# Eight attention heads and a squared-ReLU layer on one core: block products for one chunk more, scales for two passes at a time, and a planner with new numbers

## The chip, the core and the metric

The kernel runs on one core of one Trainium2 chip. The metric is the device time of one execution in microseconds. The core has a tensor engine (PE, whose weight loads, PEld, overlap its matmuls), a vector engine (DVE), a scalar engine (ACT), GpSimd (POOL) and a sync engine (SP), which here does nothing but issue DMAs. Each engine takes its instructions in the order in which the program lists them.

## The reference

Eight batches of eight heads of 576 tokens with 64 numbers each go through block-causal attention. What comes out, 4608 tokens of 512 numbers, goes through a two-layer network with a squared ReLU.

```python
scores = scale * np.matmul(q, k.transpose(0, 1, 3, 2))
mask = (pos[:, None] // 64) >= (pos[None, :] // 64)
scores = np.where(mask, scores, -1000000000.0)
scores = scores - np.max(scores, axis=-1, keepdims=True)
attn = np.exp(scores)
attn = attn / (np.sum(attn, axis=-1, keepdims=True) + 1e-09)
x = np.matmul(attn, v)            # then (8 * 576, 512)
h = x @ w_in                      # 512 -> 2048
r = np.maximum(h, 0.0)
out = (r * r) @ w_out             # 2048 -> 512
```

Everything is float32. The kernel gets near that from float16 matmuls: a number is split into a high and a low float16 part, and a product takes three matmuls (high with high, high with low, low with high).

## The kernel before, in words

**Attention.** The work is cut into 40 passes of one batch and two heads: 8 short ones (batches 0 and 1, the first three blocks of 64 queries), 8 for the other six blocks of those batches, and 24 whole ones (batches 2 to 7). For each group of query blocks a pass does scores on PE (A, tile `side`), the negated row maximum on DVE (B, `nmx`), the exponential on ACT (C, `p`, with its row sum `sm`), the sum's scaling on POOL (S), the reciprocal on DVE (R, `rs`), and the scaled rows with their split (H and L, `p_rows`), which DMAs (T) turn into `p_turned`. The product with v (G, PE, `px`) and a copy out on ACT (X, `x32`) end it. The first 12 passes (`WHOLE`) take v in float32. From the thirteenth pass on v is split too, and for that each pass finds a power of two: `front` (line 522) sums |v| along each row on ACT (fv, tile `st`), transposes the sums on PE (fa, `pm`), takes the maximum on DVE (fb, `top`), spreads it over the partitions with a matmul (fc), masks it on DVE (fd, `m`), makes the scales on POOL (fe, three instructions), and ACT and DVE write the high and low halves (vh, vl, `v16`). These tasks are put into the plan from line 1661 on; one task `load` issues the DMAs for a pass's queries, keys and values.

**The network.** The 4608 tokens are 12 chunks of 384, in the order 0, 1, 2, 4, 3, 5, 7, 6, 8, 10, 9, 11 (`turn_of`, line 781). A chunk's x is normalised (hb, xm: squares, a sum by matmul `nq`, a power of two) and split into `xt_all`. Then the first layer comes in one of two forms, which `plain(ck)` and `PLAIN` (lines 32 and 783) choose:

- The first four chunks of the order are plain (`unit`, line 932): 16 units, each of 12 matmuls with 384 columns into a PSUM tile `pair`; then a relu (pos), a square (sqr), the cast to the high half of `hidden` (top) and the remainder, its low half (rem).
- The other eight are made by block products (`group_steps`, line 1028): weights and x are cut in 2 x 2 blocks and combined as in Strassen's and Winograd's scheme, so that seven products stand for eight. There are 4 groups of 7 products, each of 12 matmuls with 192 columns into tiles `group`. Copies (c, ACT or DVE) and adds (a, DVE) put the products together in tiles `r`; then square, cast and remainder as above. A square on DVE is one instruction, on ACT two (relu, then square; for `r21`, which comes from a relu, one). The weights' combinations are made once, by `turn_steps` (line 979): for each quarter 18 steps, 10 adds and 4 remainders on POOL or DVE, 4 casts on ACT. They stand in `turned_w` and, some, in place of blocks of `w1`, so the last five steps of a quarter wait for the last plain chunk's first layer (line 1601).

The second layer (`out_steps`, line 1144) is 144 matmuls with 512 columns for each chunk, 48 for 128 tokens, in tiles `pair` or `po`; the output is scaled (ob, one instruction on DVE or two on ACT) and stored.

**Weights.** Both matrices arrive as float32 words and pass through a chain for each of 16 slices: bits (POOL), prelu (ACT, tile `wt`), join (DVE), a maximum (DVE for the first, ACT for the second), then the cast (ACT, DVE or POOL) and the low half (DVE). All of that runs beside the first passes and chunk 0.

**The order of the work.** `Plan` (line 152) decides it before anything runs. Every task has one or more engines with a cost in ns for each, the tasks it waits for, rings of buffers that it takes and frees, and a rank. `run` steps through a model of time: of the tasks that could start first on the engine that comes free first it takes the one with the lowest rank. Where a task may go to several engines, it takes the one with the lowest sum of start and cost:

```python
cost = at + queues[q] + (EASE + (SPARE if name[0] in "Dc" and "POOL" in queues else 0) if q == "DVE" else 0)
```

`DRAGS` (line 155) is by how much a task on POOL holds up DVE in that model. The constants of lines 34 to 74 and the table `SHIFTS` (line 100) move ranks. The order that comes out is written down through the helper `Queue`, whose line 124 therefore stands in every row of the profile (125 after the change): rows are told apart by tiles.

Of the kernel before, what the change touches and what calls it, by code (L numbers as in the profile page):

```python
# [19 lines left out]
P = 128  # L20
D = 64
# [10 lines left out]
PLAIN = 4  # L32
ALONE = 14
CALM = 1195.46
# [19 lines left out]
W0 = (-248.45, 10.9, 139.39, 8.21, 175.27, 11.63, 23.26)  # L54
W1 = (-30.45, -241.86, -561.58, -723.11, -96.62)
NORMS = (-3.68, -3.62)
YR = (90.87, 1.94, 1.28, -9.6)
UR = (225.07, 13.43, 15.26)
LATER = 16
EASE = 61.67  # L60
SPARE = 157.67
SLACK = 0
EARLY = 542.67
BEGIN = 281.87
FILLER = 10000
CHAIN = 488.46
FRONT = 95.73
# [4 lines left out]
TURN = (2121.43, -14.33)  # L72
# [61 lines left out]
class Lines:  # L134
# [8 lines left out]
    def behind(self, later, earlier):  # L143
# [1634 lines left out]
```

## Time and profile before

| | |
|---|---|
| three runs, median (lowest to highest) | 989.27 us (988.4 to 989.52) |
| the profiled execution | 989.28 us |
| its span (first to last instruction) | 987.5 us |
| PE busy | 956.1 us, 97% of the span |
| PEld busy | 598.8 us |
| DVE busy | 786.2 us, 80% |
| ACT busy | 606.0 us, 61% |
| POOL busy | 210.0 us, 21% |
| granted clock of PE, mean | 0.988 |
| DMA, bytes moved | 114.92 MB, 116 GB/s on average |

The first rows show busy time as a sum over each engine's instructions; an engine can be busy and another one's wait can still set the pace, so a share is no bound by itself. Idle time of an engine that isn't the bottleneck costs nothing. Matmuls are pipelined: the mean duration of one in the groups of instructions is longer than the distance from one to the next, and the cost of one in a stream is a dense stretch's length by its number of matmuls. Names of tiles stand as output<-inputs; the shapes are partitions x elements.

### The profile page before, as it was taken

The page shows a single profiled execution, that of the slowest core. Times are in us where ns is not written, and L with a number is a line of the kernel's source. Part 1 is how long each engine was busy: PE and PEld are TensorE (multiplying, and loading weights), DVE is VectorE, ACT ScalarE, POOL GpSimd, SP SyncE. Part 2 cuts the span into 40 slices and gives each one's busy share as a digit, 9 for nine tenths or more (in the row PEclk, how much of TensorE's full clock was granted, in tenths as well). Part 3 has the DMA queues.
Part 4 walks back from the last instruction along what each step waited for, and adds up shares of the span by engine and source line. Part 5 has one row for each costly group of instructions (what it writes and reads, how often), then busy time and mean ns, then how long its engine had stood idle before and what let it go on. Part 6 is the DMA issues. An engine that isn't in the chain of part 4 may idle for free.

```text
span 987.5 us, 20889 instructions
## 1 busy us (share of the span) xinstructions
PE 956.1 (97%) x8027; PEld 598.8 (61%) x8027; DVE 786.2 (80%) x1749; ACT 606.0 (61%) x1535; POOL 210.0 (21%) x354
## 2 busy tenths in 40 slices
PE   6789899999999999999999999999999999999998
PEld 5455544554554554596486586596577476496675
DVE  6798998878999669799789698899679788576361
ACT  5799963865887685565465566667566567353240
POOL 3635310002334213132022012122012011101000
PEclk9889989999999999999999999999999999999999
DMA  9835454585753713954760652945561560700001
GB/s 357 308 136 179 116 157 88 127 177 135 153 135 94 153 35 67 206 110 93 148 142 12 133 122 45 211 68 150 132 143 21 136 127 20 137 12 11 23 2 33
DMA packets 221649, 114.92 MB, mean 116 GB/s; under 512 B 195290, under 2 KB 203756, under 8 KB 221548
## 3 DMA queue, kind: packets, MB, share of 16 engines
q1 hardware_dynamic: 221548, 113.57, 48.2%
q8 instruction: 63, 1.03, 0.4%
q14 instruction: 38, 0.31, 0.1%
HBM read 58.21 MB, written 9.46 MB: 69 GB/s over the span
## 4 chain that ended last, share of the span: by engine, by line
PE 68%; DVE 13%; ACT 7%; issue 6%; DMA 3%; POOL 2%; SPq 0%; POOLq 0%; DVEq 0%; ACTq 0%
PE pair L124 33%; PE group L124 21%; PE side L124 6%; PE px L124 5%; DVE w L124 3%; DVE p_rows L124 3%; ACT p L124 2%; DVE nmx L124 2%; PE po L124 2%; ACT r L124 1%; DMA w<-in_w_in 1%; DVE _AluOpType.subtract L124 1%; DVE xt_all L124 1%; DMA hidden<-in_w_in 1%; DVE r L124 1%
## 5 line engine op out<-in xcount | busy, mean ns | idle before, releaser
L124 PE MATMUL pair<-w,hidden 128*128 128x512 f16 (+1 forms) x1680 | 380.2, 376 | 2.1 <-DVE ob L124 1.4
L124 PEld LDWEIGHTS <-hidden 128*128 128x128 f16 x1776 | 167.4, 98 | 185.3 <-issue 14.8
L124 PEld LDWEIGHTS <-w 128*128 128x128 f16 x2304 | 202.2, 98 | 71.6 <-issue 20.7
L124 ACT ACTIVATE p<-side,nmx 128x576 f32<-128x576 f32 (+8 forms) x264 | 139.7, 539 | 87.3 <-DVE nmx L124 73.1
L124 PE MATMUL group<-xt_all,w 128*128 128x192 f16 x1536 | 141.8, 246 | 0.0
L124 DVE SCALAR_TENSOR_TENSOR p_rows<-p,rs,p_rows 128x64 f16<-128x64 f32 (+6 forms) x264 | 138.2, 562 | 4.5 <-DMA p_turned<-p_rows 1.5
L124 PE MATMUL pair<-xt_all,w 128*128 128x384 f16 x768 | 136.3, 334 | 3.4 <-DVE xt_all L124 3.4
L124 DVE TENSOR_REDUCE nmx<-side 128x1 f32<-128x448 f32 (+8 forms) x288 | 123.2, 479 | 12.8 <-PE side L124 12.5
L124 ACT CAST hidden<-r 128x384 f16<-128x384 f32 x188 | 94.8, 510 | 26.4 <-DVE r L124 23.5
L124 POOL TENSOR_SCALAR sm<-sm 128x2 f32<-128x2 f32 (+2 forms) x104 | 29.1, 279 | 381.5 <-ACT p L124 373.3
L124 PE MATMUL group<-xt_all,turned_w 128*128 128x192 f16 x1152 | 108.6, 246 | 0.0
L124 PE MATMUL side<-qk 64*64 64x512 f32 (+2 forms) x480 | 95.2, 492 | 6.7 <-ACT p L124 6.1
L124 ACT ACTIVATE r<-group 128x384 f32<-128x384 f32 x100 | 48.9, 489 | 85.0 <-PE group L124 83.8
L124 PEld LDWEIGHTS <-turned_w 128*128 128x128 f16 x1152 | 95.8, 98 | 7.5 <-issue 2.0
L124 POOL TENSOR_TENSOR hidden<-r,hidden 128x384 f16<-128x384 f32 x55 | 57.9, 1053 | 195.6 <-ACT hidden L124 131.0
L124 DVE TENSOR_TENSOR hidden<-r,hidden 128x384 f16<-128x384 f32 x137 | 81.3, 599 | 16.3 <-ACT hidden L124 15.1
L124 ACT ACTIVATE p_rows<-p,rs 128x128 f16<-128x128 f32 (+9 forms) x148 | 67.6, 501 | 37.8 <-DVE rs L124 34.3
L124 PE MATMUL side<-ks,qk 64*64 64x128 f32 (+4 forms) x576 | 90.6, 420 | 0.0
L124 PE MATMUL px<-p_turned,v 128*64 128x384 f16 (+5 forms) x1168 | 70.9, 270 | 0.5 <-ACT x L124 0.2
L124 PEld LDWEIGHTS <-v 128*64 128x64 f16 x1128 | 50.6, 110 | 27.4 <-issue 16.9
L124 DVE SCALAR_TENSOR_TENSOR r<-group,r 128x384 f32<-128x384 f32 x96 | 52.9, 552 | 14.0 <-PE group L124 10.3
L124 DVE SCALAR_TENSOR_TENSOR r<-r 128x384 f32<-128x384 f32 x98 | 58.8, 603 | 3.6 <-ACT r L124 1.2
(147 smaller groups left out, 1069.3 us busy)
## 6 DMA issues: line engine op xcount, KB each, us to landing
qk<-in_qk SPq DMA_DIRECT2D x32, 576.0 KB
ks<-in_ks SPq DMA_DIRECT2D x32, 320.0 KB
vraw<-in_vm SPq DMA_DIRECT2D x30, 256.0 KB
w<-in_w_out SPq DMA_DIRECT2D x10, 512.0 KB
out<-ob SPq DMA_DIRECT2D x17, 256.0 KB
w<-in_w_in SPq DMA_DIRECT2D x8, 512.0 KB
out<-ob SPq DMA_DIRECT2D x26, 128.0 KB
hidden<-in_w_in SPq DMA_DIRECT2D x6, 512.0 KB
```

Of the source, the lines that this page charges most:

```text
L124: i = make(*a, **k)
```

## The change

1. `PLAIN` goes from 4 to 3. Chunk 4, the fourth in order, makes its first layer by block products; three plain chunks are left. The turning of the weights and the banks for `group` and `po`, which hang on the last plain chunk, now hang on the third.
2. `front` takes two passes. ACT's sums of |v| of both go into one tile of two columns (what the activation itself writes goes to a tile `unread` that nobody reads), and the transpose, the maximum, the spreading matmul, the mask and POOL's three instructions are done once for both. The two maxima are put on a diagonal, which takes DVE one instruction more. A task `vals` loads both passes' values; `load` keeps queries and keys.
3. `BIAS` adds a number to the cost by which a task of a kind chooses its engine. `DRAGS`, the planner's constants and `SHIFTS` have new values. `LOADS` has not.

```diff
-PLAIN = 4
+PLAIN = 3
 ALONE = 14
-CALM = 1195.46
+CALM = 320.1
...
-W0 = (-248.45, 10.9, 139.39, 8.21, 175.27, 11.63, 23.26)
+W0 = (88.86, 5.4, 88.8, 6.03, 149.27, 40.39, -1474.99)
...
-EASE = 61.67
-SPARE = 157.67
+EASE = 148.74
+SPARE = 438.43
+BIAS = {'D ACT': 538, 'D DVE': 451, 'D POOL': 0, 'F ACT': -454, 'F DVE': -498, 'H ACT': -16, 'H DVE': -236, 'c ACT': -55, 'c DVE': -22, 'cast ACT': -617, 'cast DVE': -587, 'cast POOL': -424, 'h ACT': 145, 'h DVE': 225, 'ob ACT': -1244, 'ob DVE': 22, 'rem DVE': 25, 'rem POOL': -380, 's DVE': 0, 's POOL': -2314, 'sq ACT': 0, 'sq DVE': 1579, 't DVE': 68, 't POOL': 9105, 'top ACT': -5174, 'top DVE': 12}
...
+def kind_of(name):
+    return "".join(c for c in name.split("_")[0] if not c.isdigit())
...
-    DRAGS = (("bits", 0.4), ("cast", 0.3), ("rem", 0.15), ("D", 0.35), ("top", 0), ("t", 0.4), ("s", 0.2))
+    DRAGS = (("bits", 0.3), ("cast", 0.2), ("rem", 0.42), ("D", 0.25), ("top", 0), ("t", 0.5), ("s", 0.55), ("fe", 0.05))
...
-                cost = at + queues[q] + (EASE + (SPARE if name[0] in "Dc" and "POOL" in queues else 0) if q == "DVE" else 0)
+                cost = at + queues[q] + BIAS.get(f"{kind_of(name)} {q}", 0) + (EASE + (SPARE if name[0] in "Dc" and "POOL" in queues else 0) if q == "DVE" else 0)
...
-        def v_sum():
-            box["st"] = small.tile([P, 1], F32, tag="st", name=f"st_{u}")
-            t["v16"] = p2.tile([P, 2, 2, 5, D], F16, tag="v16", name=f"v16_{u}")
-            nc.scalar.activation(t["v16"][:, 0, :, 0:c, :], v32, AF.Abs, accum_out=box["st"])
+        def v_sum(e):
+            t = pair[e]
+            if e == 0:
+                box["st"] = small.tile([P, 2], F32, tag="st", name=f"st_{u}")
+            c = t["chunks"]
+            nc.scalar.activation(unread[:, :, 0:c, :], t["v32"][:, :, 0:c, :], AF.Abs, accum_out=box["st"][:, e : e + 1])
...
-            nc.tensor.transpose(pm[:1, :P], box["st"], ident)
+            nc.tensor.transpose(pm[:2, :P], box["st"], ident)
...
-            box["top"] = small.tile([1, 1], BF16, tag="top", name=f"top_{u}", bufs=1)
-            nc.vector.tensor_reduce(box["top"], box["pm"][:1, :P], axis=AX.X, op=ALU.max)
+            mx = small.tile([2, 1], F32, tag="top", name=f"mx_{u}", bufs=1)
+            dg = box["dg"] = small.tile([2, 2], BF16, tag="vd", name=f"vd_{u}", bufs=1)
+            nc.vector.tensor_reduce(mx, box["pm"][:2, :P], axis=AX.X, op=ALU.max)
+            nc.vector.tensor_scalar(dg, ident[:2, :2], mx, None, op0=ALU.mult)
...
-            nc.tensor.matmul(box["pm"][:, P : P + 1], ones_bf[:1], box["top"], start=True, stop=True)
+            nc.tensor.matmul(box["pm"][:, P : P + 2], ones_bf[:2], box["dg"], start=True, stop=True)
...
-            prior = [f"vl{i - 2}"] if i - 2 >= WHOLE else [f"G{i - 4}_1"] if i > 11 else [f"G{q}" for q in range(4)]
...
+                if i - 2 >= WHOLE:
+                    prior = [f"vl{i - 2}", f"vl{i - 1}"]
+                elif i > 11:
+                    prior = [f"G{i - 4}_1", f"G{i - 3}_1"]
+                else:
+                    prior = [f"G{q}" for q in range(4)]
+                r = front_rank
+                add(f"vals{i}", "SP", 1900, prior, ahead + 1, both, size=2 * P * 2 * S * 4)
+                for e in range(2):
+                    add(f"fv{i + e}", "ACT", 740, [f"vals{i}"] + [f"fv{i}"] * e, r, go("v_sum", e))
+                add(f"fa{i}", "PE", 120, [f"fv{i}", f"fv{i + 1}"], r, go("turned"), ("x",))
```

What the new numbers do to the order is seen in the lists of instructions of each engine. Three places follow.

The first is ACT's list around the last relu of chunk 0's first layer. `r_0_f<-pair` is the relu of unit f, `r<-r` its square, `CAST hidden` its high half, `p32` an exponential of attention, `w2<-w2` the cast of a slice of the second layer's weights. Before:

```order
L124 ACTIVATE r_0_14_1408<-pair0_76 128x384
L124 ACTIVATE p32_1_0_3_4_1410,sm_1_0_3_4_1411<-side0_75,nmx_1_0_3_4_1319 128x320
L124 ACTIVATE p32_1_0_3_4_1410,sm_1_0_3_4_1411<-side0_75,nmx_1_0_3_4_1319 128x256
L124 ACTIVATE r_0_15_1422<-pair1_81 128x384
L124 ACTIVATE p32_1_1_3_8_1425,sm_1_1_3_8_1426<-side1_80,nmx_1_1_3_8_1404 128x576
L124 ACTIVATE p32_1_1_3_8_1425,sm_1_1_3_8_1426<-side1_80,nmx_1_1_3_8_1404 128x448
L124 ACTIVATE r_0_8_1143<-r_0_8_1143 128x384
L124 CAST hidden_106<-r_0_8_1143 128x384
L124 ACTIVATE r_0_9_1166<-r_0_9_1166 128x384
L124 CAST hidden_106<-r_0_9_1166 128x384
```

After:

```order
L125 ACTIVATE w2_106<-w2_106,wsc1_111 128x512
L125 ACTIVATE r_0_14_1479<-pair0_76 128x384
L125 ACTIVATE r_0_14_1479<-r_0_14_1479 128x384
L125 CAST hidden_107<-r_0_14_1479 128x384
L125 ACTIVATE w2_106<-w2_106,wsc1_111 128x512
L125 ACTIVATE r_0_15_1495<-pair1_81 128x384
L125 ACTIVATE r_0_15_1495<-r_0_15_1495 128x384
L125 CAST hidden_107<-r_0_15_1495 128x384
L125 ACTIVATE w2_106<-w2_106,wsc1_111 128x512
L125 ACTIVATE p32_1_1_3_8_1513,sm_1_1_3_8_1514<-side1_80,nmx_1_1_3_8_1461 128x576
```

Squares and casts of units 8 to 15 stood behind the last relu (those of units 8 and 9 are seen), and now stand right behind their own unit's relu, with a cast of weights behind each.

The second is DVE's list where chunk 1's x is made: `hb` is its power of two, `x32<-x32,hb` the scaling, `xt_all` the two halves. Before, the remainders of chunk 0's units (`hidden<-r,hidden`) follow:

```order
L124 TENSOR_SCALAR hb_0_1_1419<-nq_0_1_1414 128x384
L124 TENSOR_SCALAR hb_0_1_1419<-hb_0_1_1419 128x384
L124 RECIPROCAL rs_1_0_3_4_1433<-sm_1_0_3_4_1411 128x2
L124 TENSOR_SCALAR p_rows_90<-p32_1_0_3_4_1410,rs_1_0_3_4_1433 128x320
L124 TENSOR_SCALAR p_rows_90<-p32_1_0_3_4_1410,rs_1_0_3_4_1433 128x256
L124 TENSOR_TENSOR x32_94<-x32_94,hb_0_1_1419 128x1536
L124 TENSOR_REDUCE top_1_0_3_1453<-pm_1_0_3_1441 1x1
L124 CAST xt_all_103<-x32_94 128x1536
L124 TENSOR_TENSOR xt_all_103<-x32_94,xt_all_103 128x1536
L124 TENSOR_SCALAR m_1_0_3_1470<-pm_1_0_3_1441 128x1
L124 TENSOR_TENSOR hidden_106<-r_0_8_1143,hidden_106 128x384
```

After, with the last low half of the second layer's weights (`w2<-turned_w,wsc1,w2`) ahead of it:

```order
L125 SCALAR_TENSOR_TENSOR w2_106<-turned_w_103,wsc1_111,w2_106 128x512
L125 TENSOR_TENSOR sq_0_1_2_1387<-sq_0_1_2_1387 128x384
L125 SCALAR_TENSOR_TENSOR v16_1_1_3_1626<-vraw1_89,s_1_0_3_1596,v16_1_1_3_1626 128x640
L125 RECIPROCAL rs_1_2_3_8_1722<-sm_1_2_3_8_1696 128x2
L125 TENSOR_REDUCE nmx_1_2_3_7_1731<-side0_75 128x1 x2
L125 TENSOR_SCALAR nmx_1_2_3_7_1731<-nmx_1_2_3_7_1731 128x2
L125 TENSOR_SCALAR hb_0_1_1742<-nq_0_1_1724 128x384
L125 TENSOR_SCALAR hb_0_1_1742<-hb_0_1_1742 128x384
L125 SCALAR_TENSOR_TENSOR p_rows_91<-p32_1_2_3_8_1695,rs_1_2_3_8_1722,p_rows_91 128x576
L125 TENSOR_TENSOR x32_95<-x32_95,hb_0_1_1742 128x1536
L125 SCALAR_TENSOR_TENSOR p_rows_91<-p32_1_2_3_8_1695,rs_1_2_3_8_1722,p_rows_91 128x448
L125 CAST xt_all_104<-x32_95 128x1536
```

The making of chunk 1's x stood ahead of chunk 0's remainders from unit 8 on, and now stands behind all of chunk 0's remainders and all of the weights' slices.

The third is chunk 9, the eleventh in order, at the seam of its second and third groups. Before, DVE adds the products (`r<-group,r`), squares them (`r<-r`) and makes the remainders (`hidden<-r,hidden`):

```order
L124 SCALAR_TENSOR_TENSOR r11_9_1_11024<-group0_4845,r11_9_1_11024 128x384
L124 TENSOR_TENSOR hidden_106<-r12_9_0_11055,hidden_106 128x2x192
L124 TENSOR_TENSOR hidden_106<-r21_9_1_11170,hidden_106 128x2x192
L124 SCALAR_TENSOR_TENSOR r11_9_1_11024<-r11_9_1_11024 128x384
L124 SCALAR_TENSOR_TENSOR r11_9_2_11202<-group2_4847,r11_9_2_11202 128x384
L124 TENSOR_SCALAR ivs_11_11109<-ivs_11_11109 128x3
L124 SCALAR_TENSOR_TENSOR r11_9_2_11202<-r11_9_2_11202 128x384
L124 SCALAR_TENSOR_TENSOR r22_9_1_11124<-group0_4845,r22_9_1_11124 128x384
L124 SCALAR_TENSOR_TENSOR r22_9_1_11124<-r22_9_1_11124 128x384
```

After, ACT squares them, in two instructions (x2; one for `r21`, which is positive already), and casts:

```order
L125 ACTIVATE r11_9_1_11169<-r11_9_1_11169 128x384 x2
L125 CAST hidden_107<-r11_9_1_11169 128x2x192
L125 ACTIVATE r21_9_1_11316<-group1_3724 128x384
L125 ACTIVATE r21_9_1_11316<-r21_9_1_11316 128x384
L125 CAST hidden_107<-r21_9_1_11316 128x2x192
L125 ACTIVATE r22_9_1_11270<-r22_9_1_11270 128x384 x2
L125 CAST hidden_107<-r22_9_1_11270 128x2x192
L125 ACTIVATE r11_9_2_11301<-r11_9_2_11301 128x384 x2
L125 CAST hidden_107<-r11_9_2_11301 128x2x192
```

The squares of the groups left DVE for ACT; DVE keeps the adds.

## Rows read from the trace of the kernel before

**Rows 1.** Busy time by stretch, whole core; columns: stretch, length, then busy us (instructions) per engine, clock.

```profile
0.00:40.00 40.00, 28.99 (x239) 21.29 (x239) 27.92 (x79) 22.32 (x78) 18.84 (x41) 0.91 0.97 358
40.00:120.00 80.00, 71.60 (x520) 40.48 (x520) 73.33 (x160) 77.20 (x198) 35.81 (x49) 0.94 0.46 154
...
160.00:420.00 260.00, 256.29 (x1895) 133.31 (x1894) 216.50 (x480) 183.09 (x462) 60.78 (x102) 1.00 0.61 131
420.00:860.00 440.00, 438.85 (x4117) 294.65 (x4115) 368.31 (x845) 265.68 (x678) 81.14 (x145) 1.00 0.51 109
...
sum 988.00, PE 956.06 PEld 598.78 DVE 786.17 ACT 606.02 POOL 209.99; mean PE 159.34 PEld 99.80 DVE 131.03 ACT 101.00 POOL 35.00
```

**Rows 2.** Timeline of PE around 120 us; columns: start, busy us, work, [idle before, releaser].

```profile
122.14 0.16 PE L124 MATMUL pm<-top,ones_bf 1*128 1x1 bf16 x1 [1.23 <-DVE top L124]
123.00 0.32 PE L124 MATMUL pair<-xt_all,w 128*128 128x384 f16 x1 [0.71 <-DVE xt_all L124]
124.80 8.72 PE L124 MATMUL pair<-xt_all,w 128*128 128x384 f16 x35 [1.47 <-DVE xt_all L124]
```

**Rows 3.** Chain of waits, dense pieces of PE; columns: start, us, work and matmuls.

```profile
73.29 1.95 PE pair L124 x12
...
231.92 1.86 PE px L124 x30
...
417.62 2.97 PE group L124 x36
...
931.90 19.80 PE group L124 x240
...
963.39 10.36 PE po L124 x48
```

**Rows 4.** Groups of instructions, PE and weight loads; columns: count, busy us, mean ns, idle before.

```profile
L124 PE MATMUL group<-xt_all,w 128*128 128x192 f16 x1536 | 141.8, 246 | 0.0
...
L124 PE MATMUL pair<-xt_all,w 128*128 128x384 f16 x768 | 136.3, 334 | 3.4 <-DVE xt_all L124 3.4
...
L124 PEld LDWEIGHTS <-turned_w 128*128 128x128 f16 x1152 | 95.8, 98 | 7.5 <-issue 2.0
```

**Rows 5.** Timeline of PE, a transpose for v's scale among second-layer matmuls.

```profile
236.29 0.27 PE L124 MATMUL pm<-ident,st 128*1 128x128 f32 x1
236.40 1.46 PE L124 MATMUL pair<-w,hidden 128*128 128x512 f16 x6
```

**Rows 6.** Groups of instructions, the work that changes engines or place.

```profile
L124 ACT CAST hidden<-r 128x384 f16<-128x384 f32 x188 | 94.8, 510 | 26.4 <-DVE r L124 23.5
...
L124 DVE TENSOR_TENSOR hidden<-r,hidden 128x384 f16<-128x384 f32 x137 | 81.3, 599 | 16.3 <-ACT hidden L124 15.1
...
L124 DVE SCALAR_TENSOR_TENSOR r<-r 128x384 f32<-128x384 f32 x98 | 58.8, 603 | 3.6 <-ACT r L124 1.2
...
L124 POOL TENSOR_TENSOR hidden<-r,hidden 128x384 f16<-128x384 f32 x55 | 57.9, 1053 | 195.6 <-ACT hidden L124 131.0 <-PE group L124 64.0
L124 ACT ACTIVATE r<-r 128x384 f32<-128x384 f32 x103 | 53.8, 523 | 5.4 <-DVE r L124 3.2
...
L124 DVE TENSOR_SCALAR ob<-pair,uv 128x512 f32<-128x512 f32 (+1 forms) x27 | 21.5, 796 | 39.6 <-PE pair L124 39.6
...
L124 DVE TENSOR_TENSOR _AluOpType.subtract<-_AluOpType.subtract,w 128x512 f32<-128x512 f32 x21 | 15.9, 763 | 0.5
...
L124 ACT ACTIVATE wt<-w 128x512 f32<-128x512 f32 x18 | 12.0, 682 | 2.6 <-DMA w<-in_w_in 2.6
...
L124 ACT ACTIVATE ob<-pair,uv 128x512 f32<-128x512 f32 x8 | 5.5, 685 | 7.8 <-PE pair L124 7.7
...
L124 ACT ACTIVATE w<-w,wsc 128x512 f16<-128x512 f32 x2 | 1.4, 716 | 0.0
```

**Rows 7.** Timeline of ACT, chunk 0's last relu.

```profile
118.21 0.50 ACT L124 ACTIVATE r<-pair 128x384 f32<-128x384 f32 x1
```

**Rows 8.** Timeline of the end, the last output scaling.

```profile
984.27 0.54 DVE L124 TENSOR_SCALAR ob<-po,uv 128x256 f32<-128x256 f32 x1 [4.70 <-PE po L124]
```

More of the change, by code (lines that the diff above doesn't have):

```diff
@@ L1673, in plan_all @@
-            box = {}
-            def start(t=t, box=box):
-                box.update(front(t))
-            def go(name, first=False, box=box, start=start):
-                def run():
-                    if first:
-                        start()
-                    box[name]()
-                return run
-            r = front_rank
-            add(f"fv{i}", "ACT", 740, [f"load{i}"], r, go("v_sum", True), ("v16",))
-            add(f"fa{i}", "PE", 120, [f"fv{i}"], r, go("turned"), ("x",))
@@ L1689, in plan_all @@
-            add(f"fb{i}", "DVE", 210, [f"fa{i}"], r, go("largest"), ("top",))
-            add(f"fc{i}", "PE", 100, [f"fb{i}"], r, go("spread"), frees=[(f"fb{i}", "top")])
-            add(f"fd{i}", "DVE", 130, [f"fc{i}"], r, go("read"), frees=[(f"fa{i}", "x")])
-            add(f"fe{i}", "POOL", 1020, [f"fd{i}"], r, go("scales"))
+            last = [f"load{i - 1}"] if i > 8 else []
+            ahead = order.get(f"Y{i - 8}", 56 + 3 * (i - 8) if early else base - 150)
+            add(
+                f"load{i}", "SP", 900, last, ahead, lambda t=t: load_rows(t), ("qk", "ks"), size=P * (3 * S + D) * 4,
+            )
@@ new lines, in plan_all, with go, run, both @@
+            pair = passes[i : i + 2]
+            if i % 2 == 0:
+                box = {}
+                def go(name, *e, pair=pair, box=box):
+                    def run():
+                        if not box:
+                            box.update(front(pair))
+                        box[name](*e)
+                    return run
+                def both(pair=pair):
+                    for t in pair:
+                        load_values(t)
+                if i - 2 >= WHOLE:
[6 more added lines that the diff above has]
+                add(f"vals{i}", "SP", 1900, prior, ahead + 1, both, size=2 * P * 2 * S * 4)
+                for e in range(2):
+                    add(f"fv{i + e}", "ACT", 740, [f"vals{i}"] + [f"fv{i}"] * e, r, go("v_sum", e))
+                add(f"fa{i}", "PE", 120, [f"fv{i}", f"fv{i + 1}"], r, go("turned"), ("x",))
+                add(f"fb{i}", "DVE", 320, [f"fa{i}"], r, go("largest"), ("top",))
+                add(f"fc{i}", "PE", 100, [f"fb{i}"], r, go("spread"), frees=[(f"fb{i}", "top")])
+                add(f"fd{i}", "DVE", 90, [f"fc{i}"], r, go("read"), frees=[(f"fa{i}", "x")])
+                add(f"fe{i}", "POOL", 1020, [f"fd{i}"], r, go("scales"))
@@ L1693, in plan_all @@
             ready_rows = [f"load{i}"]
             slots = [(f"load{i}", x) for x in ("qk", "ks")]
-            add(f"vh{i}", "ACT", 720, [f"fe{i}"], r + (2 if early else 20), go("v_high"))
-            add(f"vl{i}", "DVE", 800, [f"vh{i}"], r + (2 if early else 20), go("v_low"))
+            add(f"vh{i}", "ACT", 720, [f"fe{i - i % 2}"], front_rank + (2 if early else 20), go("v_high", i % 2), ("v16",))
+            add(f"vl{i}", "DVE", 800, [f"vh{i}"], front_rank + (2 if early else 20), go("v_low", i % 2))
@@ L1720, in plan_all @@
                         f"G{i}_{g}", "PE", 1850 if g else 460, back + [f"vl{i}"], rank + 6, lambda t=t, g=g: products(t, g), ("x",),
[L1721 removed]
+                        frees=[(f"vh{i}", "v16")] if g else [],
                     )
```

80 lines of the change are left out of this document (42 added, 38 removed).

## The prediction

> **What bounds the kernel now.** I read the page's head first, then the table of busy time by stretch, then the timeline of the tensor engine where that table shows it idle. The profiled execution took 989.28 us, 1.8 us of it outside the 987.5 us span; the median of the three runs is 989.27, so sums made against the profile are sums against the median. The reader is to see two kernels in one in [rows 1]. From 420 to 860 us PE is busy 438.85 of 440 us: it is the bound, the other engines have room, and what PE no longer does is time won. From 40 to 120 us PE idles 8.4 of 80 us while ACT is busy 77.2 and DVE 73.3: there the pace is set by ACT and DVE, which prepare the weights beside the first attention passes. Around 120 us [rows 2] PE waits three times, 1.23 + 0.71 + 1.47 = 3.4 us, once for a scale of v and twice for chunk 1's x (all vector work), and the 35 matmuls after that take 8.72 us, 249 ns each.
>
> **The parts.**
>
> *The fourth chunk by block products.* Chunk 4 loses 16 units of 12 matmuls with 384 columns = 192, and gets 4 groups of 7 x 12 with 192 columns = 336. Dense stretches give 1.95 us for 12 and 19.80 us for 240 [rows 3]: 162.5 and 82.5 ns each. So 31.2 us go and 27.7 come: **-3.5 us** of PE. The whole busy times [rows 4], disturbed stretches included, give 192 x 136.3/768 = 34.1 and 336 x 141.8/1536 = 31.0, so -3.1: that is the other end.
>
> The Trainium skill (TensorE: Matmul & The Clock Gate, "Back-to-back issue gap") speaks against this part: it gives streams of load-and-multiply pairs some 81 ns a matmul at 128 columns and 131 at 512, and a straight line between makes 89 ns at 192 and 114 at 384, by my estimate. By that the chunk would cost 29.9 instead of 21.9 us, 8 us more. The 82.5 and 162.5 ns of this trace decide otherwise, and the sum goes by them.
>
> *v's scales by twos.* Each pass from the thirteenth on has one transpose and one spreading matmul (28 and 28); there will be 14 and 14. In a dense stretch the next matmul starts 0.11 us after the transpose (236.29 to 236.40) [rows 5]; for the spreading one I take the same. 28 fewer at 0.11: **-3.1 us**; by their full durations (14 x 0.27 [rows 5] + 14 x 0.16 [rows 2]) -6.0, the far end. I take 3.1, since PE is dense where most of them stand. GpSimd does 42 instructions instead of 84; DVE swaps 56 for 42. ACT does as many as before. The values of two passes are now loaded together once both passes before them are scaled, and one scale waits for two loads. Cover: a pass's scores, maxima, exponentials and row transposes stand between its load and its product with v. If that cover is gone, what is late next is this product, and behind it the chunk's norm. SP issues as many DMAs (379), rows and values in tasks of their own.
>
> *Work changes engines.* By the order, of the squares on DVE 98 become 6 and ACT's r<-r goes from 103 to 288; of the remainders DVE keeps 66 of 137 and GpSimd goes from 55 to 126; all output scalings go to ACT, two instructions each. With the means of [rows 6]: DVE loses 92 x 0.603 + 71 x 0.599 + 27 x 0.796 = 119 us and gets back 11 steps of turning the weights at 0.763 (8.4), and the ninth chunk's adds and splits; in all 786 to about 690, an estimate. ACT gains 185 x 0.523 = 97 and 29 output scalings of two at 0.685 (40), and hands a few splits to others: 606 to about 730. GpSimd gains 71 x 1.053 = 75 and loses 11 steps of turning and half the scales: 210 to about 275. None comes near PE's 950, so I cost this at nothing after 420 us: what hides it is PE's own 28 us (first layer) and 144 x 0.216 = 31 us (second, by the 48 in 10.36 us of [rows 3]) for every chunk.
>
> *The front is reordered.* Ahead of chunk 0's last relu ACT gets ten more casts to hidden, seven more squares and four more casts of weights: 10 x 0.510 + 7 x 0.523 + 4 x 0.716 = 11.7 [rows 6]; what else moves there takes 0.9 off. That relu starts at 118.21 today [rows 7], with ACT idle 17.7 us before 40 us and 2.8 after [rows 1]. PE's work ahead of that point is the same within a microsecond. So PE is up to **10.8 us** later there. Against it: five more preparations of weights stand early, where ACT idles (5 x 0.68 = 3.4) [rows 6]. And chunk 1's first layer comes behind the 144 second-layer matmuls of chunk 0, 31 us, and not right after its norm. So the 3.4 us of waits and the slow matmuls behind them (35 x (249 - 162.5) ns = 3.0) have no cause left. Net 10.8 - 3.4 - 6.4 = **+1.0**. Ends: -6.4 if ACT isn't the pace, +10.8 if nothing comes back.
>
> *Other waits.* PE idles 3.7 us from 160 to 420 and 1.15 from 420 to 860 [rows 1]. I leave them. Ends: -4.8, and +10 for new ones.
>
> *The end.* The last scaling is one DVE instruction of 0.54 us [rows 8] and becomes two of ACT. Two at 0.685 for twice the width [rows 6] would be 0.8 more, none is the other end; **+0.4**.
>
> Sum: 989.3 - 3.5 - 3.1 + 1.0 + 0.4 = **984.1 us**.
>
> **Rivals.**
>
> *A, the front costs nothing (faster).* For it: ACT's 17.7 idle us before 40 can take more than five instructions, and with DVE's share lighter the pace before 120 us may not be ACT's order. Against: ACT is 97% busy from 40 to 120 [rows 1]. Then 989.3 - 3.5 - 3.1 - 6.4 + 0.4 = 976.7.
>
> *B, the middle gives it back (no change).* Turning the weights for the block products must be done before the fourth chunk, not the fifth. Its window, from the last short pass's product to the first group, is 231.92 to 417.62 today, 186 us [rows 3], and about half that after, by the order. DVE's part goes from 29 steps to 40, at 0.763 [rows 6]: from 22 in 186 us (12%) to 31 in some 95 (32%). DVE is busy 216.5 of 260 us in this stretch today [rows 1], 83%; with 20% more it is full, unless the remainders that go to GpSimd make room. In-order engines that full wait on each other; 5 us of it makes 989.2. Against: 71 remainders at 0.6 leave DVE over the whole span, and PE idles only 3.7 us there with DVE at 83%.
>
> *C, ACT's order sets the front in full (slower).* If ACT stays as full as it is from 40 to 120, every microsecond put ahead of chunk 0's last relu comes out of PE, and PE, dense from there on both ways, never wins it back. If the early idle time is not filled and the waits come elsewhere: 989.3 - 6.6 + 10.8 + 0.4 = 993.9. It decides from 7 us of uncovered lag on. For it: [rows 1]; against: the waits of [rows 2] lose their cause.
>
> *D, weight loads set the pace of block products.* Each of the 336 loads its own weights, 98 ns [rows 4]; if a matmul had to wait for that, they would take 32.9 us, 1.7 more than the 31.2, not 3.5 less: 989.3. The 240 in 19.80 us are loads and all, so I give it 2 in 100. The figures of the Trainium skill (the section named above) point this way.
>
> **How the numbers follow.** Forecast 46 in 100, A 16, B 19, C 17, D 2. The measurement of this kernel tells about 0.2% (2 us) from no change. Forecast and A are faster: 0.62; B and D the same: 0.21; C slower: 0.17. The range: the forecast's own costs spread it to about 979 to 988; taking in most of A and of C it is 975 to 994.
>
> **What would show it.** Right: 3024 group matmuls at 82 to 84 ns and 576 with 384 columns; 14 transposes for v; PE busy about 6 us less in all; no slow matmuls after 120 us; chunk 0's last relu at 119 to 128 us. Wrong: that relu later than 130 us (C), or at 118 and before (A); PE idle more than 6 us between 160 and 420 us, ended by DVE or GpSimd (B); group matmuls at 95 ns or more (D). If DVE is still above 760 us, or ACT idles between 40 and 120 us, the account of the engines is wrong.

## The result, and the profile after

The change makes the kernel faster: 980.59 us (979.73 to 982.07) against 989.15 us of the kernel before on the same chips. The ratio is 0.9916, 95% interval 0.9904 to 0.9928, so 8.3 us (7.1 to 9.5). The profiled execution has a span of 977.9 us, 9.6 less than the one of before. Busy time by stretch, in the columns of [rows 1]:

```profile
0.00:40.00 40.00, 29.08 (x264) 21.51 (x265) 29.71 (x81) 26.99 (x89) 23.52 (x48) 0.96 0.97 369
40.00:120.00 80.00, 66.70 (x466) 36.06 (x466) 74.29 (x162) 75.85 (x189) 39.98 (x50) 0.91 0.51 168
120.00:160.00 40.00, 39.64 (x240) 17.97 (x240) 37.51 (x74) 32.52 (x70) 4.83 (x9) 1.00 0.65 143
160.00:420.00 260.00, 257.61 (x2112) 148.33 (x2106) 216.75 (x473) 196.10 (x484) 74.51 (x106) 1.00 0.61 124
420.00:860.00 440.00, 438.98 (x4118) 295.22 (x4109) 319.56 (x715) 332.46 (x813) 115.55 (x166) 1.00 0.49 107
...
sum 988.00, PE 946.08 PEld 603.26 DVE 716.46 ACT 724.87 POOL 276.14; mean PE 157.68 PEld 100.54 DVE 119.41 ACT 120.81 POOL 46.02
```

PE is busy 946.1 us instead of 956.1, DVE 716 instead of 786, ACT 725 instead of 606, GpSimd 276 instead of 210. PE's idle time as a whole has hardly changed (977.9 - 946.1 = 31.8 us, before 31.4): the front has more of it, the rest less. The chain of waits has the dense pieces that answer to [rows 3]:

```profile
183.29 1.95 PE pair L125 x12
...
863.71 16.83 PE group L125 x204
```

These are 162.5 ns and 82.5 ns for a matmul, the same two figures as before. The groups of instructions that answer to [rows 4, 6], and the ones of v's scales:

```profile
L125 PE MATMUL group<-xt_all,w 128*128 128x192 f16 x1728 | 159.7, 246 | 0.9 <-DVE xt_all L125 0.9
L125 ACT ACTIVATE r<-r 128x384 f32<-128x384 f32 x288 | 150.3, 522 | 17.1 <-DVE r L125 11.4
L125 POOL TENSOR_TENSOR hidden<-r,hidden 128x384 f16<-128x384 f32 x126 | 124.8, 991 | 243.9 <-ACT hidden L125 223.2 <-DVE r L125 14.6 <-PE group L125 5.3
L125 PE MATMUL group<-xt_all,turned_w 128*128 128x192 f16 x1296 | 122.1, 246 | 0.0
...
L125 PE MATMUL pair<-xt_all,w 128*128 128x384 f16 x576 | 101.3, 330 | 6.2 <-DVE w L125 5.9 <-ACT r L125 0.2
...
L125 DVE TENSOR_TENSOR hidden<-r,hidden 128x384 f16<-128x384 f32 x66 | 42.4, 649 | 40.3 <-ACT hidden L125 39.6
...
L125 PE MATMUL pm<-ident,st 128*2 128x128 f32 x14 | 3.8, 272 | 0.0
...
L125 PE MATMUL pm<-vd,ones_bf 2*128 2x2 bf16 x14 | 2.4, 172 | 0.1
```

The front has traded its waits. Those of [rows 2] are gone, and the granted clock is 1.00 from 120 to 160 us, where the kernel before had 0.91 (the stretch that is left out in [rows 1]):

```profile
120.00:160.00 40.00, 36.09 (x202) 17.44 (x203) 36.95 (x72) 18.43 (x43) 6.33 (x10) 0.91 0.37 107
```

In their place PE's timeline has one long wait, for the low half of a slice of the first weights, and the ten matmuls behind it take 338 ns each, some twice their 162.5: from 71.2 to 74.6 us the granted clock is 0.50, the lower of its two levels (1.2 of 2.4 GHz):

```profile
64.79 0.49 PE L125 MATMUL pair<-xt_all,w 128*128 128x384 f16 x2
71.23 3.38 PE L125 MATMUL pair<-xt_all,w 128*128 128x384 f16 x10 [5.95 <-DVE w L125]
```

ACT's timeline has chunk 0's last relu at 126.6 us ([rows 7]: 118.2), and the timeline of the end has two instructions of ACT where [rows 8] had one of DVE:

```profile
126.58 0.47 ACT L125 ACTIVATE r<-pair 128x384 f32<-128x384 f32 x1
```

```profile
974.12 0.47 ACT L125 ACTIVATE ob<-po,uv 128x256 f32<-128x256 f32 x1 [4.23 <-PE po L125]
974.63 0.51 ACT L125 ACTIVATE ob<-ob,uv 128x256 f32<-128x256 f32 x1
```

### The profile page after: what moved, and what is told of

It is laid out like the page before. It is cut to its first block, busy times and chain, and to the rows that moved or that the text cites. A ratio compares the mean times of both kernels' runs of the same rounds, so it can differ in the third digit from the quotient of the medians.

```text
span 977.9 us, 21279 instructions
## 1 busy us (share of the span) xinstructions
PE 946.1 (97%) x8143; PEld 603.3 (62%) x8143; DVE 716.5 (73%) x1569; ACT 724.9 (74%) x1764; POOL 276.1 (28%) x395
## 4 chain that ended last, share of the span: by engine, by line
PE 75%; DVE 9%; ACT 9%; issue 2%; DMA 2%; POOL 2%; SPq 0%; ACTq 0%; POOLq 0%; DVEq 0%
PE pair L125 36%; PE group L125 25%; PE side L125 7%; PE px L125 5%; DVE p_rows L125 3%; ACT p L125 2%; DVE w L125 2%; ACT r L125 2%; PE po L125 2%; DVE nmx L125 1%; DMA p_turned<-p_rows 1%; DVE _AluOpType.subtract L125 1%; ACT p_rows L125 1%; ACT wt L125 1%; DMA w<-in_w_in 1%
## 5 line engine op out<-in xcount | busy, mean ns | idle before, releaser
L125 POOL TENSOR_TENSOR hidden<-r,hidden 128x384 f16<-128x384 f32 x126 | 124.8, 991 | 243.9 <-ACT hidden L125 223.2
L125 ACT ACTIVATE p<-side,nmx 128x256 f32<-128x256 f32 (+8 forms) x264 | 139.5, 538 | 49.8 <-DVE nmx L125 40.9
L125 ACT ACTIVATE r<-r 128x384 f32<-128x384 f32 x288 | 150.3, 522 | 17.1 <-DVE r L125 11.4
L125 DVE SCALAR_TENSOR_TENSOR p_rows<-p,rs,p_rows 128x64 f16<-128x64 f32 (+7 forms) x264 | 145.8, 588 | 8.4 <-DMA p_turned<-p_rows 4.5
L125 DVE TENSOR_REDUCE nmx<-side 128x1 f32<-128x64 f32 (+8 forms) x288 | 123.7, 482 | 18.2 <-PE side L125 17.9
L125 PE MATMUL pair<-xt_all,w 128*128 128x384 f16 x576 | 101.3, 330 | 6.2 <-DVE w L125 5.9
L125 PE MATMUL side<-ks,qk 64*64 64x192 f32 (+4 forms) x576 | 91.6, 425 | 0.0
L125 DVE TENSOR_TENSOR hidden<-r,hidden 128x384 f16<-128x384 f32 x66 | 42.4, 649 | 40.3 <-ACT hidden L125 39.6
L125 ACT ACTIVATE p_rows<-p,rs 128x128 f16<-128x128 f32 (+10 forms) x135 | 62.1, 502 | 11.9 <-DVE rs L125 6.3
L125 DVE TENSOR_SCALAR p_rows<-p,rs 128x576 f16<-128x576 f32 (+10 forms) x151 | 64.7, 452 | 5.0 <-DMA p_turned<-p_rows 2.9
```

The costliest lines, as they stand in the source:

```text
L125: i = make(*a, **k)
```

## The experiments

Each ratio is to the kernel before on the same chip. "Against the change" is the difference of a kernel's ratio to 0.9916, in us of 989.15; it is uncertain by 1.7 to 2.7 us. Two kinds of kernel stand here. In one the planner makes a new order; in the other the order of the change, or of before, is kept instruction by instruction and only the engine or the number of some instructions is edited.

### The two parts alone, with a new order

Three plain chunks alone, in the kernel before:

```diff
-PLAIN = 4
+PLAIN = 3
```

> The kernel before with PLAIN = 3 alone; all other numbers old, scales one pass at a time. Theory (PE's work sets the time from 160 us on): the fourth chunk by block products takes 31.2 - 27.7 = 3.5 us off PE, and the order made anew adds or takes a microsecond: 985.7, within 984 to 987.5. Rival 'engines' (the gain of the change comes from taking 70 us of work off DVE, which here stays): DVE gets a ninth chunk's adds and squares besides, so 989 or more. Rival 'weight loads' (a matmul of the groups waits for its own load): 989 to 990.

Measured: 1001.07 us, ratio 1.0118 (1.0100 to 1.0137). Slower by 11.7 us: outside the theory's 984 to 987.5, inside what "engines" said, which the run with `BIAS` takes up.

The scales alone: the change's code of `front` and its tasks, all numbers of before, and of `SHIFTS` one entry less. (The line of `PLAIN` is seen against the change, that of `SHIFTS` against before.)

```diff
-PLAIN = 3
+PLAIN = 4
...
-A20 32, A21 -9.5, A32 -520, A9 -300
+A20 32, A21 -9.5, A9 -300
```

> The kernel before with v's scales for two passes at a time, four plain chunks, no BIAS, old DRAGS and old numbers; one shift (pass 32's scores) is taken out, because the planner finds no order with it. Theory (PE's work): 28 transposes and spreading matmuls fewer at 0.11 us = 3.1 us: 986.1, within 984.5 to 988. Rival 'new waits' (a scale that waits for two loads and two sums comes late for the product with v): 989 or more, with PE waiting for v16 or for the DMA of p_turned.

Measured: 1035.54 us, ratio 1.0458 (1.0443 to 1.0474). Slower by 45 us. The rows of PE's timeline from 148 to 165 us show one of the places:

```profile
149.70 0.80 PE L125 MATMUL side<-qk 64*64 64x320 f32 x2 [4.27 <-ACT p L125]
153.53 0.53 PE L125 MATMUL px<-p_turned,v 128*64 128x384 f16 x2 [2.49 <-DMA p_turned<-p_rows]
159.14 3.25 PE L125 MATMUL px<-p_turned,v 128*64 128x384 f16 x28 [5.08 <-DMA p_turned<-p_rows]
```

Here it is attention's own exponentials (`p`) and turned rows (`p_turned`) that PE waits for, and in the whole run no wait of PE of 0.3 us or more is for the halves of v. But the rival had named the DMA of `p_turned` as its other sign, and that is there: 10.5 us in five waits, where the change has 1.3 in two. The scales' chain has a part in it, for DVE, which makes these rows, stood still for the spreading matmul shortly before:

```profile
144.47 0.16 DVE L125 TENSOR_SCALAR m<-pm 128x2 int32<-128x2 int32 x1 [1.40 <-PE pm L125]
```

So a v that is scaled too late for its product is out; that the shared chain makes waits of its own in this order is not.

Three plain chunks with the change's engines (`BIAS` and `DRAGS`), ranks and scales as before:

```diff
-PLAIN = 4
+PLAIN = 3
...
+BIAS = {'D ACT': 538, 'D DVE': 451, 'D POOL': 0, 'F ACT': -454, 'F DVE': -498, 'H ACT': -16, 'H DVE': -236, 'c ACT': -55, 'c DVE': -22, 'cast ACT': -617, 'cast DVE': -587, 'cast POOL': -424, 'h ACT': 145, 'h DVE': 225, 'ob ACT': -1244, 'ob DVE': 22, 'rem DVE': 25, 'rem POOL': -380, 's DVE': 0, 's POOL': -2314, 'sq ACT': 0, 'sq DVE': 1579, 't DVE': 68, 't POOL': 9105, 'top ACT': -5174, 'top DVE': 12}
...
```

> The kernel before with PLAIN = 3 and the change's BIAS and DRAGS; ranks, shifts and single scales as before. By the order, 8 squares of r stay on DVE and 285 go to ACT, remainders are 88 on DVE and 104 on GpSimd: work on engines as in the change. The ninth chunk alone had taken 3.4 us of work off PE and cost some 14 us of new gaps, 9.6 of them between 240 and 420 us and 5 after. Theory 'room' (those gaps come from DVE, which got the chunk's adds and the weights' turning in half the time): with DVE lighter by 90 us they go, 986, within 984 to 989. Rival 'ranks' (the gaps come from an order whose ranks were made for four plain chunks): they stay, 995 to 1005.

Measured: 1013.01 us, ratio 1.0238 (1.0214 to 1.0263): 23.5 us slower than before. With DVE's load lighter the waits did not go, so "room" is out; they came out larger than "ranks" had said, too.

The change with v's scales one pass at a time (the code of before for `front` and its tasks, everything else as in the change):

> The changed kernel with v's scales one pass at a time, as before; three plain chunks, BIAS, DRAGS and all ranks as in the change, so the order is made anew. Theory (PE's work): 28 small PE instructions more, 3.0 us: 983.6, within 982 to 987. Rival 'ranks' (an order made anew with ranks that weren't made for it has gaps of its own): 990 or more, with the 3.0 lost among them.

Measured: 1007.17 us, ratio 1.0180 (1.0161 to 1.0199): 26 us against the change.

Busy time from 240 to 420 us, where the weights are turned, in the columns of [rows 1]. The kernel before and the change:

```profile
240.00:420.00 180.00, 176.31 (x1322) 93.34 (x1321) 152.28 (x331) 129.46 (x326) 50.39 (x74) 1.00 0.57 124
```

```profile
240.00:420.00 180.00, 177.61 (x1477) 106.57 (x1475) 148.83 (x316) 133.80 (x330) 50.64 (x69) 1.00 0.53 111
```

Three plain chunks alone, with the change's engines, and the change with single scales:

```profile
240.00:420.00 180.00, 168.97 (x1418) 98.68 (x1417) 163.88 (x346) 128.72 (x326) 64.31 (x84) 0.99 0.57 120
```

```profile
240.00:420.00 180.00, 166.43 (x1351) 96.67 (x1342) 149.57 (x319) 122.34 (x306) 39.65 (x64) 0.96 0.50 108
```

```profile
240.00:420.00 180.00, 167.88 (x1340) 97.41 (x1339) 138.93 (x296) 126.37 (x310) 49.34 (x71) 0.98 0.48 105
```

PE idles 3.7 and 2.4 us in the two tuned kernels, and 11.0, 13.6 and 12.1 in the other three. (For the first of the three that is 7.3 more than before, not the 9.6 that was said ahead of the run with `BIAS`.) So rival B's place is right: with three plain chunks this is the stretch that gives way. Its reason, a full DVE, is not enough. DVE is busy 164, 150 and 139 of 180 us in the three; the last has less on DVE than the change and loses as much as the others. The longest waits, one row of PE's timeline from each of the three kernels in turn, are for three kinds of work on two engines:

```profile
305.62 0.24 PE L124 MATMUL nq<-sq,ones_bf 128*128 128x192 bf16 x1 [4.10 <-DVE sq L124]
```

```profile
328.43 1.12 PE L125 MATMUL side<-qk 64*64 64x512 f32 x2 [6.68 <-ACT p L125]
```

```profile
388.37 3.61 PE L125 MATMUL pair<-w,hidden 128*128 128x512 f16 x9 [3.02 <-ACT hidden L125]
```

The first two stand behind a DVE that is full just there, 25.35 of 26 us and 8.22 of 8.4:

```profile
280.00:306.00 26.00, 21.87 (x145) 10.93 (x145) 25.35 (x40) 19.41 (x49) 13.00 (x15) 1.00 0.49 111
```

```profile
320.00:328.40 8.40, 1.09 (x12) 0.49 (x12) 8.22 (x21) 4.67 (x13) 2.21 (x3) 0.68 0.69 155
```

But the change has a DVE as full for 50 us in this stretch, and PE idles 1.1 us there:

```profile
260.00:310.00 50.00, 48.93 (x361) 26.77 (x357) 48.46 (x91) 42.52 (x105) 24.52 (x26) 1.00 0.38 84
```

We read this as lists in an order that doesn't fit: where an engine is full, what PE needs next is late if it stands behind something else, and early if it doesn't. That is argued from these rows; no run changed the order of one list alone here. All four kernels with a new order from numbers that weren't made for it were slower than before, by 12 to 45 us; neither part shows its saving that way, and the gain of a part can't be read from a new order.

### The two parts as doses, with the order kept

v's scales: the changed kernel with each of the 14 transposes and 14 spreading matmuls three times.

```diff
-            nc.tensor.transpose(pm[:2, :P], box["st"], ident)
+            for _ in range(3):
+                nc.tensor.transpose(pm[:2, :P], box["st"], ident)
...
-            nc.tensor.matmul(box["pm"][:, P : P + 2], ones_bf[:2], box["dg"], start=True, stop=True)
+            for _ in range(3):
+                nc.tensor.matmul(box["pm"][:, P : P + 2], ones_bf[:2], box["dg"], start=True, stop=True)
```

> The changed kernel, in the same order, with each of the 14 transposes and each of the 14 spreading matmuls for v's scales issued three times in a row instead of once: 56 more small PE instructions, nothing else. Theory (each costs 0.11 us of a dense PE): 56 x 0.11 = 6.2 us more than the changed kernel's 980.6: 986.8, within 985.5 to 988. Rival 'full durations' (0.27 and 0.16 each): 12.0 more, 992.6. Rival 'hidden' (they fall into gaps of PE): 980.6 to 982.

Measured: 985.85 us, ratio 0.9954 (0.9939 to 0.9969): 3.8 us against the change, and 5.3 by the medians. The median lies in the theory's 985.5 to 988, but by the ratio the dose is less than 6.2; full durations (12) and hidden (0 to 1.4) are both out. PE's timeline shows why it is less:

```profile
163.25 0.49 PE L125 MATMUL pm<-ident,st 128*2 128x128 f32 x3
163.58 0.81 PE L125 MATMUL pair<-w,hidden 128*128 128x512 f16 x3
...
166.10 0.22 PE L125 MATMUL pm<-vd,ones_bf 2*128 2x2 bf16 x3
166.26 3.41 PE L125 MATMUL pair<-w,hidden 128*128 128x512 f16 x15
```

Three transposes take 0.33 us of PE, 0.11 each. Three spreading matmuls take 0.16: the first some 0.10, each repetition 0.03. All 14 places of either kind agree with that to 0.01 us. So the dose was 28 x 0.11 + 28 x 0.03 = 3.9 us, and it came out in full, within the noise. For single ones, which the change takes away, the timeline of the changed kernel gives what was predicted (163.09 to 163.19 is 0.10):

```profile
163.09 0.17 PE L125 MATMUL pm<-vd,ones_bf 2*128 2x2 bf16 x1
163.19 3.41 PE L125 MATMUL pair<-w,hidden 128*128 128x512 f16 x15
```

The ninth chunk: 44 more matmuls where it stands.

```diff
-                        nc.tensor.matmul(
+                        for _ in range(12 if ck == 4 and fresh and name == "X" and p == 0 and i == 0 else 1):
+                            nc.tensor.matmul(
```

> The changed kernel, in the same order, with 44 matmuls more in the fourth chunk: the first matmul of each of its four groups is issued twelve times, each overwriting the one before, so nothing else changes. That gives PE back what the block products save there, 44 x 82.5 ns = 3.6 us, at four places. Theory (PE is the bound where the ninth chunk stands, so its saving is worth its full time): 984.2, within 983.3 to 985.2. Rival 'cover' (PE waits in that stretch for the turned weights or for DVE anyhow, and the saving of the ninth chunk goes into the wait): 980.6 to 982.

Measured: 985.72 us, ratio 0.9968 (0.9956 to 0.9981): 5.1 us against the change, with 3.6 inside its uncertainty and "cover" outside. PE's time in the fourth chunk is worth its full length, within the noise.

### Engines, with the order kept

The changed kernel with the groups' squares and remainders on DVE, then each alone; and the kernel before with its squares on ACT.

```diff
-                if q == "DVE":
+                if q:
                     nc.vector.scalar_tensor_tensor(r, r, 0.0, r, op0=ALU.max, op1=ALU.mult)
...
-            return lambda q="DVE": (nc.vector if q == "DVE" else nc.gpsimd).tensor_tensor(
+            return lambda q="DVE": nc.vector.tensor_tensor(
```

> The changed kernel, in the same order, with all squares of the nine group chunks on DVE (one instruction each, where ACT takes two) and all of the groups' remainders on DVE too, none on GpSimd. Theory (PE is the bound, DVE at 73% has room): within 2 us of the changed kernel's 980.6, 980 to 983. Rival 'engines' (the change's gain is DVE's relief): at least 3 us slower, 984 to 990, with PE waiting for hidden, which DVE writes, or for attention's maxima behind it.

Measured: 1000.16 us, ratio 1.0101 (1.0084 to 1.0118): 18.3 us against the change. The theory as it stood here falls.

> The changed kernel, in the same order, with only the squares of the groups put on DVE: 138 more there, at 0.6 us 83 us, one instruction for ACT's two. Squares and remainders together had cost 19.6 us. Theory 'load' (what counts is DVE's added time, 83 of 140 us): 11.6 more than 980.6, 992, within 989 to 995. Rival 'chain' (a square on DVE is one step instead of two, so the way to hidden gets shorter, and only the remainders had cost anything): 979 to 983.

Measured: 997.50 us, ratio 1.0086 (1.0067 to 1.0105): 16.8 against the change, more than either's figure.

> The changed kernel, in the same order, with only the groups' remainders taken from GpSimd to DVE: 95 more there, at 0.6 us 57 us. Theory 'load': 57 of 140 us, 8.0 more than 980.6, 988.6, within 986 to 991. Rival 'chain' (the remainders had cost all of it): 996 to 1000; and if DVE's remainder, half as long as GpSimd's, helps the second layer: 979 to 981.

Measured: 980.69 us, ratio 0.9912 (0.9897 to 0.9927): no difference. The 95 remainders cost nothing on DVE in this order, so having them on GpSimd brings nothing. The squares are all of it.

```diff
-                if q == "DVE":
+                if not q:
                     nc.vector.scalar_tensor_tensor(r, r, 0.0, r, op0=ALU.max, op1=ALU.mult)
```

> The kernel before, in its own order, with all squares of the groups on ACT (two instructions for DVE's one, 98 fewer on DVE). In the changed kernel's order the same move the other way cost 17 us. Theory 'order' (an order is made for its engines; ACT has no place kept for them here, and a group's tiles r come free later): slower than before, 992 to 1005. Rival 'relief' (DVE's load is what is paid for, in any order): faster, 984 to 988.

Measured: 1007.97 us, ratio 1.0191 (1.0175 to 1.0206): 18.9 us slower than before. The same move costs as much in one order as its opposite in the other. Busy time from 420 to 960 us, first the kernel before and the change with squares on DVE, then the change and before with squares on ACT (columns as in [rows 1]):

```profile
420.00:960.00 540.00, 538.85 (x5018) 370.81 (x5016) 428.76 (x958) 304.99 (x759) 88.24 (x152) 1.00 0.43 91
```

```profile
420.00:960.00 540.00, 527.89 (x4895) 361.87 (x4894) 424.93 (x904) 290.28 (x723) 137.64 (x184) 1.00 0.41 89
```

```profile
420.00:960.00 540.00, 538.96 (x4966) 368.55 (x4957) 358.19 (x782) 390.04 (x929) 133.29 (x183) 1.00 0.41 89
```

```profile
420.00:960.00 540.00, 524.95 (x4840) 355.39 (x4839) 368.88 (x841) 370.23 (x912) 79.82 (x151) 1.00 0.43 91
```

Each pair has the same load on DVE (429 and 425, 358 and 369 us), and within each pair one kernel lets PE idle 1 us and the other 12 or 15. The load as a whole is not what decides. The waits of PE from 420 us on in the two that lose, the changed kernel with squares on DVE, then the kernel before with squares on ACT (total, times, longest):

```profile
PE side L125 <- ACT p L125: 5.1, 6, 1.6
PE group L125 <- DVE r L125: 2.9, 9, 0.7
PE group L125 <- ACT r L125: 2.2, 3, 0.8
```

```profile
PE group L124 <- ACT r L124: 6.5, 11, 1.5
PE group L124 <- DVE r L124: 2.8, 6, 0.6
```

They are many and short. In the second most are for tiles `r`; in the first as much time goes to attention's `p`. As we read them, a copy, an add or a row maximum that PE needs next stands behind a square that the order had counted for the other engine. The means over the stretch hide how full the engines are locally: of the first kernel's 20 gaps of PE over 0.2 us, 17 stand behind 5 us in which DVE was busy 94% or more, as in this row, in which the longest of them begins:

```profile
437.00:442.00 5.00, 4.39 (x39) 3.07 (x36) 5.00 (x8) 1.60 (x5) 2.16 (x3) 1.00 0.00 0
```

But the kernel before has a DVE as full about as often (95% or more in 35 of the stretch's 108 pieces of 5 us, here in 40) and only 2 such gaps. So it is, as we read it, what stands in the list when DVE is full that makes the difference.

### The front

Three instructions moved ahead in DVE's list, so that the 5.95 us wait ends earlier, and the last two scalings back on DVE. (The planner's list is collected first, and written after the moves.)

```diff
+MOVES = [('low0_2', 'join0_14'), ('cast0_3', 'join1_1'), ('low0_3', 'join1_1')]
...
-            if q == "ACT":
+            if q == "ACT" and w > 256:
                 nc.scalar.activation(ob, box["po"], AF.Copy, scale=uv[:, 0, t : t + 1])
```

> The changed kernel with three instructions moved in DVE's list and its last two output scalings on DVE: the low half of the first weights' slice 2, and slice 3's cast and low half, stand ahead of the joins of the second weights that PE waited for at 65 to 71 us; the last two scalings are one DVE instruction each. Theory (the 5.95 us wait is an order of DVE, not a lack of it): 3 to 6 us come back, 975 to 978. Rival 'full' (DVE and ACT are 93 to 95% busy from 40 to 120 us, so what comes earlier for one unit makes the next one late): 979.5 to 981.

Measured: 982.96 us, ratio 0.9938 (0.9926 to 0.9951): 2.2 us slower than the change. The wait is gone, and a longer one stands right behind that unit, in PE's timeline:

```profile
66.40 2.11 PE L128 MATMUL pair<-xt_all,w 128*128 128x384 f16 x12
75.94 1.12 PE L128 MATMUL side<-qk 64*64 64x512 f32 x2 [7.42 <-ACT p L128]
```

"Full" holds, and a little more. The row maximum that this exponential needs starts on DVE 3.6 us later than in the changed kernel (68.86), 2.0 of it by the three moved instructions, and DVE had no time to spare: it was busy 12.86 us of the 13 from 62 to 75 us.

```profile
72.50 0.81 DVE L128 TENSOR_REDUCE nmx<-side 128x1 f32<-128x320 f32 x2
```

Ten casts to hidden twice, for 5.1 us more on ACT:

```diff
-            (nc.scalar.copy if q == "ACT" else nc.vector.tensor_copy)(g[:, 0], box["r"])
+            for _ in range(2 if q == "ACT" and ck == 0 and 2 <= f < 12 else 1):
+                (nc.scalar.copy if q == "ACT" else nc.vector.tensor_copy)(g[:, 0], box["r"])
```

> The changed kernel, in the same order, with ten more instructions on ACT ahead of chunk 0's last relu: the cast to hidden of units 2 to 11 is issued twice, the second time over the same values. That is 10 x 0.510 = 5.1 us of ACT between about 73 and 118 us. Theory (from 40 us to chunk 0's last relu ACT's list sets the pace, so what stands there comes out of PE's time): 5.1 more, 985.7, within 984.3 to 987; the last relu moves from 126.6 to about 131.7. Rival 'front costs nothing' (other engines or the DMAs set the pace there): 980.6 to 982, the last relu within 1.5 us of 126.6.

Measured: 984.22 us, ratio 0.9956 (0.9943 to 0.9970): 4.0 us against the change, near the 5.1 and outside "costs nothing". ACT's timeline has the last relu 6.9 us later than the changed kernel's 126.58:

```profile
133.43 0.47 ACT L125 ACTIVATE r<-pair 128x384 f32<-128x384 f32 x1
```

Some of the 6.9 is from before the dose begins: in the first 40 us this execution had a granted clock of 0.83, where the changed kernel's had 0.96 (busy time of that stretch):

```profile
0.00:40.00 40.00, 30.16 (x237) 22.29 (x237) 26.19 (x73) 24.27 (x81) 21.91 (x41) 0.83 0.97 372
```

## Why the prediction was right, and where not

The forecast was 984.1 us and faster, the range 975 to 994; it is 980.6. Step by step:

- **The ninth chunk, -3.5 us.** Right. The counts are 3024 and 576, at 82.5 and 162.5 ns in dense stretches of both kernels, and the dose of 44 matmuls there was worth its 3.6 us, within the noise. Rival D is out. The Trainium skill's figures for such pairs (TensorE: Matmul & The Clock Gate, "Back-to-back issue gap") don't hold here either: at 512 columns it gives some 131 ns, and [rows 3] has 10.36 / 48 = 0.216 us; the straight line between its two figures, by which block products would have lost, is the prediction's own.
- **v's scales by twos, -3.1 us.** Right: 28 instructions at 0.11 and 0.10 make 2.9, beside the 3.1, and the dose came out in full.
- **Work changes engines, nothing.** Right in the sum, and the busy times are near (DVE 716 for 690, ACT 725 for 730, GpSimd 276 for 275). DVE has more than forecast because its instructions take longer: a remainder there 649 ns where it took 599 [rows 6], and over all shapes that both kernels have some 23 us (an estimate, from their means in the two traces). But the reason, "none comes near PE's 950", isn't enough. With DVE at 80% of the span, as before, squares on an engine that the order hadn't counted on cost 17 and 18 us, and with DVE at 73%, the other way, 19. That the move costs nothing because the order was made for it is what these runs point to; no run kept the order of before with all the new engines.
- **The front, +1.0 us.** The mechanism was right: the last relu moved by 8.4 us (predicted 10.8 - 3.4 = 7.4), and the waits of [rows 2] and the slow matmuls behind them went. In the rows of the stretches, PE's idle time and what it loses at the lower level of its clock (an estimate: busy time by the missing share of the clock) give:
  - From 40 to 120 us PE idles 13.3 us instead of 8.4 and loses 6.0 instead of 4.3, +6.6 (predicted 7.4). It does other work ahead of that relu (102.1 us for 99.3), which I had counted as the same.
  - From 120 to 160 us it idles 0.4 instead of 3.9 and loses nothing instead of 3.2, -6.8 (predicted -6.4).
  - In the first 40 us it idles as much and loses 1.2 instead of 2.6, -1.5, which was not forecast.

  Net -1.7 for +1.0: this is the term that was mis-sized, by 2.7 us, and with the -3.0 of the clock in it PE's busy time falls by 10.0 us and not by about 6. The -1.5 can't be put down to the change. The clock of the first 40 us was 0.96 in this execution, and 0.83, 0.87, 0.87, 0.91, 0.96 and 0.96 in the six others whose order is the same there (all runs from the changed kernel with the order kept, but for the front's moves). Over whole runs, too, the span by the missing share of the clock is 11.5 us for the kernel before (mean of 32 runs), 9.8 for the change (4) and 10.2 for 21 runs with the change's front, 1.3 to 1.7 less and not 3.0. Without it the front is -0.2.

  Rival C's premise holds (the dose on ACT's list came out at 4.0 of 5.1), though PE's longest wait there, 5.95 us, is ended by DVE and not by ACT. Its outcome doesn't hold, since what came back after 120 us is as much as what was lost ahead of it.
- **Other waits, nothing.** From 160 to 420 us PE idles 2.4 us for 3.7, -1.3, the second part of what I missed. Rival B didn't come. Its stretch is where each of the other new orders with three plain chunks left PE idle for 11 to 14 us, in two of them behind a full DVE; but the change has DVE as full there without such waits, so a full DVE alone does not do it.
- **The end, +0.4 us.** Right: from the start of the last scaling to the end of the span it was 3.23 us and is 3.78, +0.5.

With these: -3.5 - 3.1 - 1.7 - 1.3 + 0.5 = -9.1, beside 9.6 in the two spans; without what the clock happened to be in the first 40 us it is -7.6, beside 8.3 (7.1 to 9.5) in the runs.

No kernel here beat the changed one.

What stays open is which of the planner's numbers hold the stretch from 240 to 420 us together. No run took them apart one by one; each new order moved most of the instructions at once.

## What to carry to other kernels

Where an engine is dense, count its instructions in both forms by dense stretches of the trace: that sum, 6.6 us here, is most of the 8.3 that the change delivered, and doses in a fixed order bear it out. Moving work off an engine with room brings nothing by itself, and a move that the order doesn't know of can cost 17 to 19 us (the squares) or nothing (the remainders). So test a part of such a change with the order held still; a new order from old numbers measures the numbers.

## What was not expected

- In-order lists are sensitive at a mean load far below full: with equal DVE load, 79% of the stretch, PE idles 1 us or 12 from 420 to 960 us. Locally DVE is full again and again in both kernels; what stands in its list there differs. (GpSimd's load differs too, 88 and 138 us; the remainders' run speaks against that as the cause.)
- DVE slows beside GpSimd without any wait being recorded. In the changed kernel's trace the 47 remainders on DVE that no instruction on GpSimd overlaps take 557 ns on average; the 16 that GpSimd covers for more than half of their time take 938. That is what makes the mean 649, and not the number of remainders on GpSimd: only one of the 16 lies beside one of those. The time of the kernel was the same with and without those.
- A small matmul repeated back to back costs PE 0.03 us after the first one's 0.10 (the 2x2 spreading matmul, above), so a dose by repetition can weigh less than the instruction that it stands for.
